# A dynamic convolution and SwiGLU kernel on one core: the part ahead of the loop recorded anew, in one fixed order for every engine

## The chip, the cores and the metric

The kernel runs on one core of a Trainium2 chip. Its time is the device time of one execution in microseconds (us), lower is better. The kernel before takes 1240.89 us as the median of 3 runs (1240.53 to 1242.09).

## The reference, cut to what matters

```python
# x (4, 4096, 192), weight_gen (4, 4096, 8, 7), float32
w = softmax(weight_gen, axis=-1)                      # 7 taps for each of 8 heads
x_pad = concat([zeros(B, 6, D), x], axis=1)
attn[b, s, h, :] = sum_k w[b, s, h, k] * x_pad[b, s + k, h, :]
x = attn.reshape(16384, 192)
xn = x / sqrt(mean(x * x, axis=-1) + 1e-6) * rms_g
g, val = xn @ w_gate, xn @ w_val                      # (192, 1536) each, float64 in memory
out = (g * sigmoid(g) * val) @ w_out                  # (1536, 192), float64 in memory
```

## The kernel before

**Blocks.** The 16384 tokens are cut into 32 blocks of 512 (4 tokens on each of 128 partitions). Four blocks share one load group: `xg` holds the group's tokens, `wt` its tap weights. For each block `conv` multiplies the shifted `xg` by a tap seven times (`tmp`) and sums (`acc`), takes the mean square (`junk`, `ssq`, `rs`), scales (`xn`) and splits the result into two 16-bit parts (`sp`). `trans` turns `sp` round with a transposing DMA into `tt`, and two more DMAs copy the halves of `tt` crosswise into `tu`. All DMAs but one small pair are issued by SyncE (SP), in one order.

**Stage 1 and stage 2.** `s1_mm(i, c)` is a chunk: 18 matmuls of TensorE (PE), which run in pairs, give 128 columns of gate (`pg`) and value (`pv`) for block i. ScalarE (ACT) takes the Silu of `pg` (`sg`), VectorE (DVE) multiplies by `pv` (`hf`), ACT and GpSimd (POOL) split `hf` into two 16-bit halves `hh`. There are 12 chunks in a block. `s2_mm` multiplies `hh` by the split `wo` into `po`; a block has 12 units of it, 4 chunks deep each. All PSUM tiles (`acc` on PE, `pt`, `pg`, `pv`, `po`) share eight buffers.

**Weights.** `w_gate` and `w_val` arrive as float64 in five slices k of 1, 2, 2, 3 and 4 chunks (loads `s0` to `s4`, buffers `rawa`, `rawb`), `w_out` in `wost`. `decode` makes float32 of them in four steps (`hf` scaled, `lo` shifted, two combining steps on DVE), ACT squares them, PE sums the squares into `pt`, DVE makes power-of-two scales, ACT and DVE then write the high and low 16-bit halves into `wm` and `wo`.

**What sets the order.** Everything up to the loop is recorded as the string `START` calls sixteen generators; a letter advances one of them, a dot issues the next load of `LOADS`. That covers the convolutions of blocks 0 to 2, all weights, 24 chunks (blocks 0 and 1) and stage 2 of block 0. In that part only SP is held to the recorded order (`manual_schedule`); the other engines' order is Tile's choice. The loop `for i in range(2, NB)` is written with DVE and PE held to the recorded order; the chunk (2, 0) is its first matmul.

Of the kernel before, what the change touches and what calls it, by code (L numbers as in the profile page):

```python
# [18 lines left out]
P = 128  # L19
R = 16  # L20
# [5 lines left out]
LOADS = ("w0", "w1", "s0", "x0", "s1", "x1", "s2", "s3", "x2", "s4")  # L26
START = (
    "..aaaa.aa.aa.aba.gapbbagab.gbcgbcabgcp.cpccpcgccacaccaca.daacaadgg.agabgegaadcgedddceddc"
    "gdggaagbggeeagaeeggebebgebbegfgbdagefbebdeeefecjbfiiggfdgfjjgegffekcfbgkkkbkdeekcpdfffjk"
    "ffbfjfphdjjdfjjjdjcjfjkjjdfcjjhhhdlhbehfhdhjfphldiplhkphjihkjpilkfmhjbilkhpkhjmhlhkhphkk"  # L30
    "ihidkhhiinphkmmnnhhnnphlnnhpmkphmkpkhjmlmjmkpkhpkmmhmphmhnmmolppllmoplmpmnppohpmpihohohp"
    "mhhohhhnomhnmhhnnhhnnmhhnmhhnhnnhnnnooooonni"
# [19 lines left out]
def tile_dynamic_conv_swiglu(  # L52
# [44 lines left out]
    ident = const.tile([P, P], F16, name="ident")  # L97
# [82 lines left out]
    normed = set()  # L180

    def conv(i, halves=False):

# [3 lines left out]
        parts = []  # L187
        b = 0
        for n, mul in ((2, nc.vector), (2, nc.gpsimd)) if halves else ((J, nc.vector),):
            pe = b > 0  # L190
            if pe:
                acc = ps1.tile([P, n, D], F32, tag="pr", name="acc")
            else:
                acc = p_c.tile([P, J, D], F32, tag="acc", name="acc")[:, 0:n, :]
            parts.append((b, b + n, mul, pe, acc))
            b += n
        for k in range(K):
            for a, b, mul, pe, acc in parts:
# [14 lines left out]
                if pe:
# [4 lines left out]
                elif k:  # L218
                    yield mul.tensor_tensor(out=acc, in0=acc, in1=dst, op=ALU.add)  # L219
        ssq = p_s.tile([P, J], F32, tag="ssq", name="ssq")  # L220
        junk = p_s.tile([P, D], BF16, tag="junk", name="junk")
        for a, b, mul, pe, acc in parts:
# [11 lines left out]
        for a, b, mul, pe, acc in parts:  # L234
            yield nc.vector.tensor_tensor(  # L235
                out=xn[:, a:b, :], in0=acc,
                in1=rs[:, a:b].unsqueeze(2).to_broadcast([P, b - a, D]), op=ALU.mult,
            )
        normed.add(i)
# [3 lines left out]
        low = nc.vector if i < 2 else nc.gpsimd  # L243
# [47 lines left out]
    def s1_evac(i, c, pair):  # L291
        pg, pv = pair
# [5 lines left out]
        if (i, c) in POOL_HIDDEN:  # L298
            nc.scalar.activation(out=hf_of[i, c], in_=pv, func=AF.Copy, scale=cs1[:, c : c + 1])
            yield nc.gpsimd.tensor_tensor(out=hf_of[i, c], in0=hf_of[i, c], in1=sg, op=ALU.mult)  # L300
        else:
            yield nc.vector.scalar_tensor_tensor(  # L302
                out=hf_of[i, c], in0=pv, scalar=cs1[:, c : c + 1], in1=sg, op0=ALU.mult, op1=ALU.mult
            )
# [28 lines left out]
    def s2_evac(i, t):  # L333
# [4 lines left out]
        nc.scalar.activation(out=lo, in_=pt[:, D:], func=AF.Identity, scale=so[:, 1:2])  # L338
# [14 lines left out]
    def decode(raw, how):  # L353
# [24 lines left out]
        if how[2] == "p":  # L378
            yield nc.scalar.activation(out=hf, in_=hf, func=AF.Sign)
            yield nc.gpsimd.tensor_tensor(out=hf, in0=hf, in1=lo.bitcast(F32), op=ALU.mult)  # L380
        else:
            yield nc.vector.scalar_tensor_tensor(
                out=hi, in0=hi, scalar=-0x80000000, in1=lo, op0=ALU.bitwise_and, op1=ALU.bitwise_or
            )
# [27 lines left out]
    def prep_gate_val(k):  # L412
        raw = raws.pop(k)
        a, b = (v * P for v in SL[k])
        n = b - a
        sq = p_d.tile([P, 3, 4 * P], BF16, tag="sq", name="sq", bufs=2)
        for m in range(3):
            yield from decode(raw[:, m, :], DECODE[k][m])
            yield nc.scalar.activation(
                out=sq[:, m, 0:n], in_=upper(raw[:, m, :]).bitcast(F32), func=AF.Square,  # L420
                scale=g_sb[:, m : m + 1], bias=eps, accum_out=ssq_w[:, k, m : m + 1],
            )
# [4 lines left out]
        sums = [
            [(by, ssq_w[:, k, m : m + 1]) for m in range(3)] for by in (rows[:, 0, :], rows[:, 1, :], same)
        ]
        for c in range(c0, c1):  # L430
            f = slice((c - c0) * P, (c - c0 + 1) * P)
            for h in range(2):
                sums.append([(sq[:, m, f], big[:, h : h + 1]) for m in range(3)])
        for q, terms in enumerate(sums):
            for t, (a_, b_) in enumerate(terms):
                nc.tensor.matmul(
                    pt[:, q : q + 1], a_, b_, start=(t == 0), stop=(t == len(terms) - 1)
                )
        scales(pt[:, 0:w], sc[:, o : o + w], isc[:, o : o + w], -XE)
# [5 lines left out]
        yield nc.vector.scalar_tensor_tensor(  # L445
# [3 lines left out]
        nc.gpsimd.tensor_tensor(  # L449
# [374 lines left out]
```

## Time and profile before

| what | value |
|---|---|
| median of 3 runs | 1240.89 us |
| the profiled execution, its own time | 1243.09 us |
| its span, first to last instruction | 1241.2 us |
| busy PE, DVE, ACT, POOL | 95%, 69%, 53%, 48% of the span |
| mean granted TensorE clock | 0.977 |

The profiled execution is 1.9 us longer than its span, and 2.2 us longer than the median. The busy shares are means over a start of some 150 us and a loop of some 1090 us, which have different limits; they have to be read stage by stage.

### The profile page before, as it was taken

How to read it: one execution, taken by the hardware profiler on the slowest of the kernel's cores; microseconds unless marked ns; L12 is line 12 of the kernel's file. 1: busy time of each engine (PE TensorE's matmuls, PEld its weight loads, DVE VectorE, ACT ScalarE, POOL GpSimd, SP SyncE). 2: the span in 40 equal slices, each digit the busy share in tenths (PEclk: the TensorE clock that was granted, in tenths of full speed). 3: DMA queues.
4: the chain of work that ended last, by engine and by line, in shares of the span. 5: the costliest groups of instructions: out<-in, count | busy, mean ns of one | idle time of the engine just before them, and what ended most of it. 6: DMA issues, size and time to landing. Idle time of an engine off the chain costs nothing.

```text
span 1241.2 us, 24390 instructions
## 1 busy us (share of the span) xinstructions
PE 1173.1 (95%) x10141; PEld 630.9 (51%) x10141; DVE 852.3 (69%) x1163; ACT 662.5 (53%) x1320; POOL 596.0 (48%) x525
## 2 busy tenths in 40 slices
PE   3468998989999999999999999999999999999998
PEld 1223554545555555555555555555555555555554
DVE  8893467667776677777776767777776777776532
ACT  3675553464455555555556555565556645555543
POOL 6335333444454455544555445544554555544442
PEclk9579999999999999999999999999999999999999
DMA  9421240111311133111310122111311111111010
GB/s 210 114 55 27 83 123 13 27 39 39 124 27 18 35 90 72 40 39 39 111 29 25 39 68 95 40 40 39 98 32 35 39 40 40 39 39 39 6 34 27
DMA packets 68086, 67.34 MB, mean 54 GB/s; under 512 B 52492, under 2 KB 55052, under 8 KB 67080
## 3 DMA queue, kind: packets, MB, share of 16 engines
q1 hardware_dynamic: 67912, 65.79, 19.7%
q8 instruction: 79, 1.29, 0.4%
q14 instruction: 31, 0.25, 0.1%
q0 software_dynamic: 64, 0.00, 0.0%
HBM read 28.03 MB, written 12.58 MB: 33 GB/s over the span
## 4 chain that ended last, share of the span: by engine, by line
PE 73%; issue 3%; DVE 2%; ACT 2%; POOL 1%; DVEq 0%; POOLq 0%
PE pg L283 46%; PE po L325 17%; PE po L328 8%; PE pv L283 2%; DVE hf L302 2%; ACT sg L296 1%; ACT hh L310 1%; POOL rs L232 0%; DVE tmp L210 0%; POOL hh L311 0%; DVE xn L235 0%; ACT sp L242 0%; ACT L296 0%; DVE ot L339 0%; ACT lo L338 0%
## 5 line engine op out<-in xcount | busy, mean ns | idle before, releaser
L311 POOL TENSOR_TENSOR hh<-hf,hh 128x512 f16<-128x512 f32 x384 | 448.3, 1168 | 457.0 <-ACT hh L310 457.0
L283 PEld LDWEIGHTS <-wm 64*128 64x128 f16 x6912 | 346.0, 95 | 448.0 <-issue 63.0
L283 PE MATMUL pg<-tt,wm 64*128 64x512 f16 x1920 | 489.7, 382 | 13.2 <-ACT sg L296 12.1
L302 DVE SCALAR_TENSOR_TENSOR hf<-pv,cs,sg 128x512 f32<-128x512 f32 x382 | 286.5, 750 | 301.8 <-ACT sg L296 210.9
L283 PE MATMUL pv<-tu,wm 64*128 64x512 f16 x1920 | 484.7, 381 | 0.0
L310 ACT ACTIVATE hh<-hf 128x512 f16<-128x512 f32 x384 | 242.0, 630 | 356.6 <-DVE hf L302 354.7
L283 PE MATMUL pv<-tt,wm 64*128 64x512 f16 x1536 | 401.1, 382 | 13.7 <-ACT sg L296 6.4
L283 PE MATMUL pg<-tu,wm 64*128 64x512 f16 x1536 | 400.2, 381 | 0.7 <-DMA tu<-tt 0.6
L325 PE MATMUL po<-wo,hh 128*128 128x384 f16 x1536 | 379.3, 326 | 0.7 <-DVE wo L496 0.7
L328 PE MATMUL po<-wo,hh 128*128 128x192 f16 x1536 | 376.4, 246 | 0.0
L296 ACT ACTIVATE sg<-pg,isc 128x512 f32<-128x512 f32 x384 | 257.6, 671 | 24.6 <-PE pv L283 24.6
L325 PEld LDWEIGHTS <-hh 128*128 128x128 f16 x1536 | 150.2, 98 | 111.2 <-issue 13.6
L219 DVE TENSOR_TENSOR acc<-acc,tmp 128x768 f32<-128x768 f32 (+1 forms) x192 | 197.6, 1029 | 0.8
L210 DVE TENSOR_TENSOR tmp<-xg,wt 128x768 f32<-128x768 f32 (+1 forms) x192 | 187.9, 981 | 0.0
L328 PEld LDWEIGHTS <-hh 128*128 128x128 f16 x1536 | 150.3, 98 | 0.7 <-issue 0.7
L339 DVE SCALAR_TENSOR_TENSOR ot<-po,so,lo 128x192 f32<-128x192 f32 x128 | 52.8, 413 | 59.7 <-ACT lo L338 59.3
L232 POOL TENSOR_TENSOR rs<-rs,mhalf 128x4 f32<-128x4 f32 x32 | 42.7, 1333 | 86.6 <-DVE rs L228 86.1
L338 ACT ACTIVATE lo<-po,so 128x192 f32<-128x192 f32 x128 | 49.8, 409 | 46.6 <-PE po L328 42.0
L242 ACT ACTIVATE sp<-xn 128x768 f16<-128x768 f32 x32 | 27.0, 844 | 76.1 <-DVE xn L235 76.1
L224 ACT ACTIVATE junk<-acc 128x192 bf16<-128x192 f32 x128 | 46.0, 360 | 34.5 <-DVE acc L219 32.1
L244 POOL TENSOR_TENSOR sp<-xn,sp 128x256 f16<-128x256 f32 x30 | 21.9, 731 | 62.3 <-ACT sp L242 62.3
L247 POOL TENSOR_TENSOR sp<-xn,sp 128x512 f16<-128x512 f32 x30 | 50.1, 1670 | 0.0
(94 smaller groups left out, 348.3 us busy)
## 6 DMA issues: line engine op xcount, KB each, us to landing
tu<-tt SPq DMA_DIRECT2D x64, 192.0 KB, 2.9
out_dram<-ot SPq DMA_DIRECT2D x31, 384.0 KB, 3.0
xg<-in_x_dram SPq DMA_DIRECT2D x7, 1536.0 KB, 8.1
wt<-in_weight_gen_dram SPq DMA_DIRECT2D x7, 448.0 KB, 8.2
wost<-in_moe_w_out_dram SPq DMA_DIRECT2D x1, 2304.0 KB, 9.2
xg<-in_x_dram SPq DMA_DIRECT2D x4, 576.0 KB, 4.2
xg<-in_x_dram SPq DMA_DIRECT2D x4, 504.0 KB, 5.3
xg<-in_x_dram SPq DMA_DIRECT2D x2, 384.0 KB, 11.3
```

What stands on the lines that cost most here:

```text
L210: yield mul.tensor_tensor(out=dst.rearrange("p j (h c) -> p (j h) c", h=H), in0=xk, in1=wk, op=ALU.mult)
L219: yield mul.tensor_tensor(out=acc, in0=acc, in1=dst, op=ALU.add)
L247: yield low.tensor_tensor(out=sp[:, :, D + L :], in0=xn[:, :, 0:P], in1=sp[:, :, 0:P], op=ALU.subtract)
L283: mm = nc.tensor.matmul(pt, wm[h, grp, wpart, f], xT[i][half != m][h, q], start=(n == 0), stop=(n == 8))
L296: yield nc.scalar.activation(out=sg, in_=pg, func=AF.Silu, scale=isc[:, o : o + 1])
L302: yield nc.vector.scalar_tensor_tensor(out=hf_of[i, c], in0=pv, scalar=cs1[:, c : c + 1], in1=sg, op0=ALU.mult, op1=ALU.mult)
L310: yield nc.scalar.activation(out=hid[i][:, 0, c, :], in_=hf, func=AF.Copy)
L311: yield nc.gpsimd.tensor_tensor(out=hid[i][:, 1, c, :], in0=hf, in1=hid[i][:, 0, c, :], op=ALU.subtract)
L325: mm = nc.tensor.matmul(pt, hid[i][:, 0, n, c], wo[:, n, :], start=(n == 0), stop=False,)
L328: nc.tensor.matmul(pt[:, 0:D], hid[i][:, 1, n, c], wo[:, n, 0:D], start=False, stop=(n == NC - 1),)
L338: nc.scalar.activation(out=lo, in_=pt[:, D:], func=AF.Identity, scale=so[:, 1:2])
L339: nc.vector.scalar_tensor_tensor(out=ot[i][:, t, :], in0=pt[:, 0:D], scalar=so[:, 1:2], in1=lo, op0=ALU.mult, op1=ALU.add,)
```

## The change

For blocks 0 and 1 `conv` no longer halves the block between DVE (products and sums) and POOL (products, summed by PE). DVE makes all seven products over the whole block, and PE sums both halves through the identity matrix `ident32`, two matmuls of 128x384 in float32 for each tap. `decode` has no POOL steps any more, and one fixed list says which of its steps ACT takes. The generators become finer: each third of a weight slice, the high parts, the low parts and the two halves of each evacuation are streams of their own, so that one letter of `START` is about one instruction of one engine. All five engines are held to the recorded order. Two chunks whose `hf` product went to POOL go to DVE; the low split of block 2 goes from POOL to DVE. The loop's code is the same.

```diff
-LOADS = ("w0", "w1", "s0", "x0", "s1", "x1", "s2", "s3", "x2", "s4")
+LOADS = ("w0", "x0", "s0", "s1", "w1", "s2", "x1", "s3", "s4", "x2", "wo")
 START = (
-    "..aaaa.aa.aa.aba.gapbbagab.gbcgbcabgcp.cpccpcgccacaccaca.daacaadgg.agabgegaadcgedddceddc"
...
+    "...aa.aa.a.a..AAdffdffAfeedAeidiAhhighdihiAhAbllbkjebglgAbAAAbeAbksjgAgoBAsmoAmBtttAnTnA"
...
+DECODE = "aa da dd ad aa aa aa aa aa aa aa aa aa aa ad dd aa aa aa".split()
...
-    def conv(i, halves=False):
+    def conv(i, pe=False):
...
-        for n, mul in ((2, nc.vector), (2, nc.gpsimd)) if halves else ((J, nc.vector),):
...
+        if pe:
+            halves = [ps1.tile([P, n, D], F32, tag="pr", name="acc") for _ in range(2)]
+            parts = ((0, n, halves[0]), (n, J, halves[1]))
...
+        for k in range(K):
...
+            yield nc.vector.tensor_tensor(
+                out=dst.rearrange("p j (h c) -> p (j h) c", h=H), in0=xk, in1=wk, op=ALU.mult
+            )
             if pe:
...
+                for a, b, acc in parts:
                     nc.tensor.matmul(
                         acc.rearrange("p j d -> p (j d)"), ident32,
-                        dst.rearrange("p j d -> p (j d)"), start=(k == 0), stop=(k == K - 1),
+                        dst[:, a:b, :].rearrange("p j d -> p (j d)"),
+                        start=(k == 0), stop=(k == K - 1),
                     )
...
-        low = nc.vector if i < 2 else nc.gpsimd
+        low = nc.vector if i < 3 else nc.gpsimd
...
-        if (i, c) in POOL_HIDDEN:
-            nc.scalar.activation(out=hf_of[i, c], in_=pv, func=AF.Copy, scale=cs1[:, c : c + 1])
-            yield nc.gpsimd.tensor_tensor(out=hf_of[i, c], in0=hf_of[i, c], in1=sg, op=ALU.mult)
...
-            eng = nc.vector if how[0] == "d" else nc.gpsimd
-            yield eng.tensor_single_scalar(out=hf, in_=hf, scalar=2.0**-112, op=ALU.mult)
+            yield nc.vector.tensor_single_scalar(out=hf, in_=hf, scalar=2.0**-112, op=ALU.mult)
...
-        if how[2] == "p":
-            yield nc.scalar.activation(out=hf, in_=hf, func=AF.Sign)
-            yield nc.gpsimd.tensor_tensor(out=hf, in0=hf, in1=lo.bitcast(F32), op=ALU.mult)
...
+        "t": each((high_gate_val, k, m) for k in range(NS) for m in range(3)),
+        "T": each((low_gate_val, k, m) for k in range(NS) for m in range(3)),
...
+        "S": each((s1_mm, i, c) for i, c in both),
+        "O": each((s2_mm, 0, *unit(u)) for u in range(NC)),
+    }
+    streams["E"], streams["F"] = in_two(s1_evac, both)
+    streams["H"], streams["L"] = in_two(s1_split, both)
...
-    with tc.manual_schedule(engines={mybir.EngineType.SP}):
+    with tc.manual_schedule(engines={
+        mybir.EngineType.SP, mybir.EngineType.DVE, mybir.EngineType.PE,
+        mybir.EngineType.Activation, mybir.EngineType.Pool,
+    }):
         for ch in START:
```

The first place is DVE at the first convolution. Before, from its first product on, the half block is multiplied and added here (`tmp`, `acc`), while POOL multiplies the other half:

```order
L210 TENSOR_TENSOR acc<-xg,wt 128x384
L210 TENSOR_TENSOR tmp<-xg,wt 128x384 x2
L219 TENSOR_TENSOR acc<-acc,tmp 128x384
L210 TENSOR_TENSOR acc<-xg,wt 128x384
L219 TENSOR_TENSOR acc<-acc,tmp 128x384
L210 TENSOR_TENSOR tmp<-xg,wt 128x384 x2
```

Now, on the same engine and from the same product on:

```order
L191 TENSOR_TENSOR tmp<-xg,wt 128x768 x2
L342 TENSOR_SCALAR rawa<-rawa 128x128
L351 TENSOR_SCALAR rawa<-rawa 128x128
L354 SCALAR_TENSOR_TENSOR rawa<-rawa 128x128
L357 SCALAR_TENSOR_TENSOR rawa<-rawa 128x128
L191 TENSOR_TENSOR tmp<-xg,wt 128x768
```

The sums are gone from DVE, its products are twice as wide, and the decoding steps of slice 0 stand between them.

The second place is SP from the load of slice 3 (`rawb`, 384 wide) to the load of `w_out`. Before, all slices are issued ahead of the first transpose:

```order
L409 DMA rawb<-in_moe_w_val_dram 64x3x384
L151 DMA xg<-in_x_dram 128x1536
L409 DMA rawb<-in_moe_w_gate_dram 64x3x512
L409 DMA rawb<-in_moe_w_val_dram 64x3x512
L259 DMA_TRANSPOSE tt<-sp 128x12x128
L158 DMA wt<-in_weight_gen_dram 128x896
L262 DMA tu<-tt 64x1536
L263 DMA tu<-tt 64x1536
L466 DMA wost<-in_moe_w_out_dram 128x12x192
```

Now the fourth slice (512 wide) and the rest of `xg` stand behind block 0's transpose and its two copies:

```order
L384 DMA rawb<-in_moe_w_val_dram 64x3x384
L149 DMA wt<-in_weight_gen_dram 128x896
L242 DMA_TRANSPOSE tt<-sp 128x12x128
L245 DMA tu<-tt 64x1536
L246 DMA tu<-tt 64x1536
L384 DMA rawb<-in_moe_w_gate_dram 64x3x512
L384 DMA rawb<-in_moe_w_val_dram 64x3x512
L142 DMA xg<-in_x_dram 128x1536
L452 DMA wost<-in_moe_w_out_dram 128x12x192
```

So the block's own transpose no longer has the last slice in front of it, and the last slice waits for it.

The third place is SP a little later, between the copies of block 1 and the first store. Before, block 2's transpose stands ahead of the next group's load (`xg`, 128x1152 and 128x3072):

```order
L259 DMA_TRANSPOSE tt<-sp 128x12x128
L262 DMA tu<-tt 64x1536
L263 DMA tu<-tt 64x1536
L142 DMA xg<-in_x_dram 128x1152
L151 DMA xg<-in_x_dram 128x3072
L347 DMA out_dram<-ot 128x768
```

Now the load stands ahead of it:

```order
L133 DMA xg<-in_x_dram 128x1152
L142 DMA xg<-in_x_dram 128x3072
L242 DMA_TRANSPOSE tt<-sp 128x12x128
L245 DMA tu<-tt 64x1536
L246 DMA tu<-tt 64x1536
L326 DMA out_dram<-ot 128x768
```

The load of the next group has moved ahead of block 2's transpose and copies. In both programs this load goes into the buffer of `wost`, so it waits until the last `wo` is written.

## Rows read from the trace of the kernel before

**Rows 1.** Windows: us, then each engine's busy time (instructions), granted PE clock, DMA share, GB/s.

```profile
0.00:53.30 53.30, 17.56 (x112) 8.54 (x112) 44.58 (x100) 22.54 (x69) 28.90 (x43) 0.79 0.71 161
53.30:89.80 36.50, 26.09 (x182) 10.32 (x179) 35.91 (x60) 25.52 (x54) 13.97 (x11) 0.75 0.30 87
89.80:147.50 57.70, 51.34 (x396) 25.87 (x396) 23.17 (x41) 34.69 (x73) 27.41 (x24) 0.91 0.17 52
147.50:345.00 197.50, 186.01 (x1585) 102.70 (x1585) 139.78 (x174) 96.90 (x188) 82.61 (x72) 0.98 0.20 60
400.00:1200.00 800.00, 800.00 (x7084) 429.79 (x7081) 560.72 (x723) 436.34 (x850) 403.62 (x342) 1.00 0.18 48
```

**Rows 2.** Waits of PE from 0 to 147.5: us in total, times, longest.

```profile
PE pt L436 <- ACT sq L419: 19.2, 7, 9.3
PE acc L214 <- POOL tmp L210: 16.5, 7, 13.8
```

**Rows 3.** Timeline of PE: start, duration, first matmuls of chunks and of stage 2.

```profile
53.35 0.61 PE L283 MATMUL pg<-tt,wm 64*128 64x512 f16 x1
...
57.17 0.63 PE L283 MATMUL pg<-tt,wm 64*128 64x512 f16 x1
...
59.38 0.38 PE L283 MATMUL pg<-tt,wm 64*128 64x512 f16 x1
...
61.33 0.38 PE L283 MATMUL pg<-tt,wm 64*128 64x512 f16 x1
...
89.89 0.39 PE L283 MATMUL pg<-tt,wm 64*128 64x512 f16 x1 [1.01 <-ACT wm L456]
...
147.57 0.39 PE L283 MATMUL pg<-tt,wm 64*128 64x512 f16 x1
...
155.44 0.34 PE L325 MATMUL po<-wo,hh 128*128 128x384 f16 x1
...
167.31 0.39 PE L283 MATMUL pg<-tt,wm 64*128 64x512 f16 x1
```

**Rows 4.** Timeline of DVE: start, duration.

```profile
18.14 2.35 DVE L210 TENSOR_TENSOR tmp<-xg,wt 128x384 f32<-128x384 f32 x2
...
43.20 0.54 DVE L210 TENSOR_TENSOR tmp<-xg,wt 128x384 f32<-128x384 f32 x1
43.67 0.55 DVE L375 SCALAR_TENSOR_TENSOR rawb<-rawb 128x384 int32<-128x384 int32 x1
...
127.52 3.03 DVE L496 SCALAR_TENSOR_TENSOR wo<-wost,ws,wo 128x192 f16<-128x192 f32 x7 [0.86 <-ACT wo L493]
```

**Rows 5.** Groups of POOL from 0 to 40: count, busy us, mean ns, idle before.

```profile
L210 POOL TENSOR_TENSOR tmp<-xg,wt 128x384 f32<-128x384 f32 x14 | 15.3, 1119 | 0.6 <-DMA xg<-in_x_dram 0.6
```

**Rows 6.** Timeline of SP's issues: start, duration.

```profile
17.30 0.60 SPq L409 DMA_DIRECT2D rawb<-in_moe_w_val_dram  x1
...
41.28 1.53 SPq L259 DMA_TRANSPOSE tt<-sp  x1
...
45.61 0.60 SPq L263 DMA_DIRECT2D tu<-tt  x1
```

**Rows 7.** DMA issues from 0 to 160: KB each, us from issue to landing.

```profile
xg<-in_x_dram SPq DMA_DIRECT2D x1, 1536.0 KB, 8.9
tu<-tt SPq DMA_DIRECT2D x6, 192.0 KB, 3.0
...
rawb<-in_moe_w_val_dram SPq DMA_DIRECT2D x1, 768.0 KB, 21.9
```

**Rows 8.** Timeline of PE: one float32 matmul of 128x384 (two records) each.

```profile
18.99 0.91 PE L214 MATMUL acc<-tmp,ident 128*128 128x384 f32 x2
...
32.81 1.63 PE L214 MATMUL acc<-tmp,ident 128*128 128x384 f32 x2
```

**Rows 9.** Groups of DVE from 400 to 1200: count, busy us, mean ns, idle before.

```profile
L302 DVE SCALAR_TENSOR_TENSOR hf<-pv,cs,sg 128x512 f32<-128x512 f32 x276 | 207.0, 750 | 206.2 <-ACT sg L296 132.1 <-issue 74.1
L219 DVE TENSOR_TENSOR acc<-acc,tmp 128x768 f32<-128x768 f32 x132 | 136.8, 1036 | 0.3
```

More of the change, by code (lines that the diff above doesn't have):

```diff
@@ L220, in conv @@
         ssq = p_s.tile([P, J], F32, tag="ssq", name="ssq")
         junk = p_s.tile([P, D], BF16, tag="junk", name="junk")
-        for a, b, mul, pe, acc in parts:
+        for a, b, acc in parts:
             for j in range(a, b):
@@ L233, in conv @@
         xn = p_c.tile([P, J, D], F32, tag="xn", name="xn", bufs=1)
[L234 to L235 removed]
+        for a, b, acc in parts:
+            mul = nc.vector.tensor_tensor(
                 out=xn[:, a:b, :], in0=acc,
@@ L410, in load_gate_val, with square_gate_val, scale_gate_val @@
         raws[k] = raw
[L412 to L422, printed above, removed]
+    sqs = {}
+    def square_gate_val(k, m):
+        n = (SL[k][1] - SL[k][0]) * P
+        raw = raws[k][:, m, :]
+        yield from decode(raw, DECODE[3 * k + m])
+        if k not in sqs:
+            sqs[k] = p_d.tile([P, 3, 4 * P], BF16, tag="sq", name="sq", bufs=2)
+        yield nc.scalar.activation(
+            out=sqs[k][:, m, 0:n], in_=upper(raw).bitcast(F32), func=AF.Square,
+            scale=g_sb[:, m : m + 1], bias=eps, accum_out=ssq_w[:, k, m : m + 1],
+        )
+    def scale_gate_val(k):
         c0, c1 = SL[k]
+        sq = sqs.pop(k)
         w = 3 + 2 * (c1 - c0)
@@ L426, in prep_gate_val @@
         pt = ps1.tile([P, TB], F32, tag="pr", name="pt")
[L427 to L435, printed above, removed]
+        for q, by in enumerate((rows[:, 0, :], rows[:, 1, :], same)):
+            for m in range(3):
                 nc.tensor.matmul(
-                    pt[:, q : q + 1], a_, b_, start=(t == 0), stop=(t == len(terms) - 1)
+                    pt[:, q : q + 1], by, ssq_w[:, k, m : m + 1], start=(m == 0), stop=(m == 2)
                 )
+        for c in range(c1 - c0):
+            for m in range(3):
+                nc.tensor.matmul(
+                    pt[:, 3 + 2 * c : 5 + 2 * c], sq[:, m, c * P : (c + 1) * P], big,
+                    start=(m == 0), stop=(m == 2),
+                )
+        yield
         scales(pt[:, 0:w], sc[:, o : o + w], isc[:, o : o + w], -XE)
@@ L613, in s2_unit, with each, in_two, head @@
         if u % 3 == 2:
-            s2_evac(i, u // 3)
+            run(s2_evac(i, u // 3))
         return mm
-    done = {}
-    def need(ch, n):
-        while done.get(ch, 0) < n:
-            step(ch)
+    def each(steps):
+        for f, *args in steps:
+            r = f(*args)
+            if hasattr(r, "__next__"):
+                yield from r
+            else:
+                yield
+    def in_two(make, keys):
+        begun = {}
+        def head():
+            for key in keys:
+                begun[key] = make(*key)
+                yield next(begun[key])
+        def tail():
+            for key in keys:
+                run(begun.pop(key))
+                yield
+        return head(), tail()
@@ L748, in tile_dynamic_conv_swiglu @@
+    assert not left and all(next(gen, 0) == 0 for gen in streams.values())
     if NG > 1:
```

272 lines of the change are left out of this document (91 added, 181 removed).

## The prediction, made before the changed kernel ran

> **What bounds the kernel now.** I read the busy time by stretches first, since the page's means mix a start and a loop [rows 1]. From 400 to 1200 us PE is busy all 800 us at full clock: the loop is bound by PE, nothing there is left to win, and the change does not touch it. From 147.5, where the loop's first chunk starts, to 345 PE loses 197.5 - 186.0 = 11.5 us: in its first blocks VectorE is late. The rest is lost ahead of the loop. Of the first 147.5 us PE works 17.6 + 26.1 + 51.3 = 95.0, and part of that at half clock (0.79, 0.75 and 0.91 granted).
>
> What it waits for stands in the waits of that stretch [rows 2]: 19.2 us for squares of weights (ACT), 16.5 us for POOL's products. Neither engine is itself full there. DVE is: 44.6 of the first 53.3 us, and 35.9 of the next 36.5 [rows 1]. ACT's squares wait for decoded weights, which DVE makes. So DVE's work decides when the first and the ninth chunk can run.
>
> The timeline of PE gives four marks [rows 3]: the first chunk starts at 53.35, the ninth (the first one that needs weight slice 4) at 89.89, the loop at 147.57, and the end comes 1241.2 - 147.57 = 1093.6 after that. A chunk takes 57.17 - 53.35 = 3.82 us at half clock and 61.33 - 59.38 = 1.95 at full, stage 2 of a block 167.31 - 155.44 = 11.87. At full clock the way from first chunk to loop would be 24 x 1.95 + 11.87 = 58.7 us; it takes 94.2. The start is worth up to 35 us there, and the 53 us ahead of it more.
>
> Why is DVE so full? Two of its products of half a block beside POOL's take 2.35 us, one alone 0.54 [rows 4]. POOL multiplies 14 times, 15.3 us in all, 1.12 each [rows 5]: a DVE operation beside one of POOL's takes about as long as POOL's. The Trainium skill says in "SBUF — State Buffer", section "SBUF: two separate sides", that a DVE operation with two SBUF inputs and a GpSimd one that reads SBUF lock each other out for a whole instruction. Rows 4 and 5 agree.
>
> **The change, step by step.** I carry the four marks over to the new order.
>
> *To the first chunk.* POOL's 15.3 us and the doubled DVE operations go. DVE makes seven products of 128x768 for a block: 0.95 each, from 2 x 0.54 less one start (in the loop operations of that size average 1.04 beside POOL [rows 9]). It loses all sums: before, six adds and seven products of half width, each at 0.54 to 1.2. Loads are the other limit. Before, 7164 KB are down at 17.3 + 21.9 = 39.2 us [rows 6, 7], 183 KB/us. The first tokens now stand right behind the first taps, with 1068 KB down at some 6 to 9 us instead of behind 1788; the eighth product, block 1's first, needs the second tokens, 3710 KB, at 20 to 22. From 8.5 us DVE's list up to block 0's last low split has nine such products (8.6 us) and some forty decoding and softmax steps of 0.1 to 0.75 (about 9.6, sized by width from the 0.55 of a 384-wide step [rows 4]); the squares, root and scaling of block 0 add about 3 of waiting. That is 29.7 for the transpose, which was issued at 41.28 [rows 6]. To the end of its two copies it took 45.61 + 3.0 - 41.28 = 7.3 [rows 6, 7]. Slice 4 no longer stands before it. The first chunk: **37.0** instead of 53.35, 16.3 less. Bounds 33 (no waiting) and 43 (the loads set each step).
>
> *PE's price.* Sums on PE are not free. A tap of a block is two matmuls; one takes 0.91 alone at full clock and 1.63 at half, and their difference of 0.72 is its time without the latency [rows 8], so 1.44 us for a tap, 2.6 to 2.9 at half clock. For block 0 that follows the products with little to spare: `tmp` has two buffers, so at half clock PE would hold up DVE from the third product on. For block 1 ten of the fourteen stand between the first chunk and the fourth, where PE is on the path: 7.2 us.
>
> *First to ninth chunk.* PE has three chunks and ten sums up to block 1's last sum: 3 x 1.95 + 7.2 = 13.1, plus about 4 for its first microseconds at half clock (3.82 for 1.95, twice). That sum is there at 54. Behind it ACT, now in a fixed order, must do block 1's squares, three squares of slice 4 and six high parts (5.5 us) before the third Silu at 60; DVE follows with its products, the scales of slice 4 and the low parts at 67.5. The ninth chunk: **67.5** instead of 89.89; the stretch is 30.5 against 36.5, 6.0 less. Slice 4 is issued at about 35, behind the copies, and is down at about 45 (1536 KB at 183 KB/us, 8.4, and two for the latency): ahead of its first use at 47, so its move costs nothing; if it comes later, every microsecond over two counts. Bounds 26 and 38.
>
> *Ninth chunk to the loop.* Sixteen chunks and stage 2 need 16 x 1.95 + 11.87 = 43.1 at full clock; before, 57.7. What stands beside them on DVE has grown, since `w_out`'s decoding and block 2's convolution now lie here: up to `wo` 17 products `hf` (12.8), 12 operations of the convolution (12.4) [rows 9], 8 steps on `wost` (as `hf`, 6.0), and the small ones, about 33 when the start-to-start overlap is taken off (43.67 - 43.20 = 0.47 for an operation of 0.54 [rows 4]). So `wo` starts at 67.5 + 33.5 = 101, where PE would be ready at 67.5 + 15 x 1.95 = 96.8: 4.2 to 5 lost. Twelve `wo` take 12 x 0.43 = 5.2 [rows 4], alongside PE's first units.
>
> Here the third place of the order costs. The next group's `xg` waits for the last `wo`, at 106, and needs 8.9 [rows 7]; block 2's transpose, ahead of it before, is behind it now, and its low split stands on DVE behind the first `ot`. Transpose and copies are ready some 18.5 after `wo` starts, PE is done with stage 2 after 14.2: 3.5 to 4 lost (nothing if the transfers share the queue well). The stretch is 43.1 + 5 + 4 = 52, the loop starts at **119.5** instead of 147.57: 5.7 less. Bounds 45 and 64.
>
> *The loop.* Same code, same order on PE and DVE; its early losses of 11.5 come from DVE's order behind `hf`, not from the start's end. 0, bounds -4 and +4.
>
> **Sum:** -16.3 - 6.0 - 5.7 = -28 us. Against the profiled execution's 1243.1 that is 1215.1; the median lies 2.2 lower, so 1240.9 - 28 = **1213 us**.
>
> **Rivals.**
>
> *POOL's lock moves (0.12).* POOL's 24 splits of 1.2 us for blocks 0 and 1 now fall on a full DVE. Its 14 operations of the convolution would take 1.9 instead of 0.95 if each met one: 13 us more, so `wo` at 114 and about **1226**. Against it: in the loop, with POOL busy 404 of 800 us, such adds average 1.04, not 1.9 [rows 1, 9].
>
> *The start opens further (0.06).* If loads are quicker, the ninth chunk runs at 60 and neither `wo` nor the transpose holds PE, the loop starts at 60 + 43.1 = 103 and the time is about **1197**. For it: DVE loses more work than I count on. Against it: ACT has some 33 us of its own in the last stretch.
>
> *PE stays at half clock (0.05), the slower side.* From first chunk to loop PE has 58.7 + 7.2 = 66 us at full clock, 132 at half. From 37 on, with 12 us of waits, the loop would start at 37 + 12 + 66(1 + f), f the share of that work at half clock: 115 for none, 148 for f = 0.5, 181 for all; slower than before above one half. At f = 0.65 the time is **1252**. For it: between 53.3 and 89.8 the clock was 0.75 with PE working 26 of 36.5 us, about half at 1.2 GHz [rows 1]. Against it: with 51 of 57.7 us at work it was 0.91, and PE's waits get shorter. The Trainium skill ("TensorE: Matmul & The Clock Gate", section "What's actually happening") has throttling as the default state, which activity releases; the trace agrees in rows 3, 3.82 to 1.95 within one chunk of steady work. By that rule this rival needs waits as frequent as before.
>
> *The order is broken by one late item (0.02): no change.* With every engine in a fixed order, a late `wost` stands in ACT's queue before slice 4's high parts and holds Silu, chunks and DVE. It is due at about 55 and needed at 60; it takes 28 + 5 us of delay to lose all the gain.
>
> **How the numbers follow.** My forecast holds 0.75: gains of 17 to 39, 1202 to 1224, from the bounds of the three stretches, which will not all fall on one side. 8 in 10 are within **1202 to 1226**, with the contention case at its upper end. A difference of 0.2% (2.5 us) is about what a measurement of this kernel can tell. Faster: 0.75 + 0.12 + 0.06 = 0.93; the same 0.02; slower 0.05.
>
> **What would show it.** The first chunk near 37, POOL nearly idle up to 45, DVE products of 128x768 at 0.95 in the first 40 us; the ninth chunk near 67 behind a third Silu that waited for block 1's squares; `wo` near 101; a PE wait for `tt` or `tu` at the loop's start; the same 11 to 12 us of PE waits in the 200 us behind that. I am wrong on the cause if DVE's products there are still near 1.2 a half block, if the first chunk comes after 45, or if the loop loses other than before.

## The result, and the profile after

The changed kernel takes 1220.68 us (median of 4 runs, 1219.51 to 1221.45) against 1241.04 for the one before (4 runs): ratio 0.9834, 95% interval 0.9817 to 0.9851, 20.4 us less. The direction and the range (1202 to 1226) held; the gain is three quarters of the 28 us forecast. The profiled execution took 1221.45 us with a span of 1219.7, 21.5 less than the span before.

The marks of the prediction are the first matmuls of the first chunk, of the ninth and of the loop, and the end of the span. The table has the first of them and the stretches between:

| mark or stretch (us) | before | predicted | after |
|---|---|---|---|
| first chunk | 53.35 | 37.0 | 35.78 |
| first to ninth chunk | 36.54 | 30.5 | 32.75 |
| ninth chunk to loop | 57.68 | 52 | 53.87 |
| loop to end of span | 1093.6 | 1093.6 | 1097.3 |

Windows of after, cut at its own marks; columns as in [rows 1]:

```profile
0.00:35.70 35.70, 18.27 (x78) 9.85 (x79) 27.16 (x64) 19.11 (x56) 5.43 (x23) 0.86 0.77 164
35.70:68.50 32.80, 28.99 (x202) 13.16 (x203) 26.61 (x55) 23.39 (x50) 6.32 (x8) 0.84 0.55 157
68.50:122.40 53.90, 47.48 (x399) 23.99 (x396) 47.27 (x68) 40.71 (x93) 30.29 (x22) 0.97 0.26 63
122.40:320.00 197.60, 185.93 (x1547) 100.63 (x1549) 136.54 (x170) 94.36 (x183) 81.25 (x71) 0.96 0.21 62
400.00:1175.00 775.00, 775.00 (x6856) 417.97 (x6854) 543.63 (x702) 422.50 (x827) 391.50 (x331) 1.00 0.18 48
```

The loop from 400 us is as full of PE as before. Ahead of the first chunk DVE works 27.2 us instead of 44.6, and POOL, whose products [rows 5] are gone, 5.4 instead of 28.9. The third row is the one to stop at: DVE is now busy 47.3 of 53.9 us (before, 23.2 of 57.7), so it is as full there as PE.

The five largest waits of PE up to the loop; columns as in [rows 2]:

```profile
PE acc L196 <- DVE tmp L191: 13.8, 4, 8.0
PE pv L266 <- DVE hf L281: 3.9, 3, 3.1
PE pt L409 <- ACT sq L396: 3.3, 2, 3.1
PE pv L266 <- DMA tu<-tt: 2.5, 1, 2.5
PE pg L266 <- DVE wm L443: 1.5, 1, 1.5
```

The 19.2 us for squares have shrunk to 3.3. The 13.8 for products lie ahead of the first chunk, where PE has nothing else. What costs is new: `hf` (3.1 in one piece), block 0's copies (`tu`), for which PE stands inside the first chunk, the low parts of slice 4 (`wm`), and, on the far side of the loop's start, block 2's transposed tiles. PE's timeline at the marks:

```profile
68.53 0.38 PE L266 MATMUL pg<-tt,wm 64*128 64x512 f16 x1
...
70.56 0.39 PE L266 MATMUL pg<-tt,wm 64*128 64x512 f16 x1 [1.45 <-DVE wm L443]
...
122.40 0.39 PE L266 MATMUL pg<-tt,wm 64*128 64x512 f16 x1 [0.66 <-DMA tt<-sp]
...
125.15 0.37 PE L266 MATMUL pv<-tu,wm 64*128 64x512 f16 x1 [1.50 <-DMA tu<-tt]
125.99 0.37 PE L266 MATMUL pg<-tu,wm 64*128 64x512 f16 x1 [0.46 <-DMA tu<-tt]
```

Stage 2 of block 1 starts at 134.47, so the loop's first four chunks take 12.1 us where they took 7.9 (147.57 to 155.44 in [rows 3]). These 4.2 us, less 0.5 by which the rest of the loop is shorter, are the +3.7 of the table's last line.

### The profile page after: what moved, and what is told of

Read it like the earlier page. It is cut to its first block, busy times and chain, and to the rows that moved or that the text cites. A ratio compares the mean times of both kernels' runs of the same rounds, so it can differ in the third digit from the quotient of the medians.

```text
span 1219.7 us, 24318 instructions
## 1 busy us (share of the span) xinstructions
PE 1176.7 (96%) x10133; PEld 633.1 (52%) x10133; DVE 849.4 (70%) x1147; ACT 662.9 (54%) x1322; POOL 569.2 (47%) x499
## 4 chain that ended last, share of the span: by engine, by line
PE 74%; issue 3%; DVE 2%; ACT 2%; POOL 1%; DVEq 0%; POOLq 0%
PE pg L266 47%; PE po L304 17%; PE po L307 8%; PE pv L266 2%; DVE hf L281 2%; ACT sg L279 1%; ACT hh L289 1%; POOL rs L215 0%; DVE tmp L191 0%; POOL hh L290 0%; DVE xn L218 0%; ACT sp L225 0%; ACT L279 0%; DVE ot L318 0%; ACT lo L317 0%
## 5 line engine op out<-in xcount | busy, mean ns | idle before, releaser
L290 POOL TENSOR_TENSOR hh<-hf,hh 128x512 f16<-128x512 f32 x384 | 452.8, 1181 | 437.6 <-ACT hh L289 437.6
L191 DVE TENSOR_TENSOR tmp<-xg,wt 128x768 f32<-128x768 f32 x194 | 193.0, 996 | 7.0 <-PE acc L196 5.6
L202 DVE TENSOR_TENSOR acc<-acc,tmp 128x768 f32<-128x768 f32 x180 | 188.4, 1047 | 0.8
L215 POOL TENSOR_TENSOR rs<-rs,mhalf 128x4 f32<-128x4 f32 x32 | 43.1, 1346 | 110.2 <-DVE rs L211 109.7
## 6 DMA issues: line engine op xcount, KB each, us to landing
xg<-in_x_dram SPq DMA_DIRECT2D x2, 384.0 KB, 10.2
```

The source lines that it names most:

```text
L191: yield nc.vector.tensor_tensor(out=dst.rearrange("p j (h c) -> p (j h) c", h=H), in0=xk, in1=wk, op=ALU.mult)
L202: yield nc.vector.tensor_tensor(out=acc, in0=acc, in1=dst, op=ALU.add)
L290: yield nc.gpsimd.tensor_tensor(out=hid[i][:, 1, c, :], in0=hf, in1=hid[i][:, 0, c, :], op=ALU.subtract)
```

## The experiments

Each kernel is the changed one with the edit shown. "The theory" is the first case of an expectation, "the rival" the other. Three things limit a fine comparison. Runs of one kernel spread over 0.5 to 5.6 us. The marks come from one execution of each kernel, which need not be a middle one: that of e2 is the slowest of its four, that of e6 the fastest. And the first chunk came between 33.3 and 35.8 us in the profiled executions that have the same code up to there (after, e1, e3, e7, e10); the later load of slice 0 landed 6.4 to 8.4 us after its issue in them. So stretches from the first chunk on are compared beside the times. The kernel before, run beside each group on the same chip, had medians of 1240.6 to 1242.2; the ratios given are against these. The marks of all runs:

| run | time, median us | first chunk | to ninth | to loop | loop to end |
|---|---|---|---|---|---|
| after | 1220.68 | 35.78 | 32.75 | 53.87 | 1097.3 |
| e1 load behind the transpose | 1215.36 | 33.33 | 32.64 | 53.14 | 1093.2 |
| e2 four `tmp` | 1218.14 | 34.52 | 30.79 | 56.66 | 1097.2 |
| e3 no POOL splits | 1211.07 | 34.44 | 33.32 | 44.58 | 1097.2 |
| e4 free order | 1226.89 | 34.66 | 33.10 | 63.35 | 1093.6 |
| e5 POOL multiplies half | 1220.14 | 34.05 | 31.00 | 55.12 | 1097.1 |
| e6 slice 4 first | 1220.28 | 35.06 | 32.23 | 54.27 | 1094.1 |
| e7 = e1, four splits late | 1214.72 | 33.51 | 32.98 | 54.03 | 1092.1 |
| e8 convolution of before | 1220.47 | 38.22 | 29.73 | 55.45 | 1095.3 |
| e9 load order of before | 1225.15 | 38.58 | 33.31 | 54.47 | 1097.2 |
| e10 = e1, loop's products held | 1211.45 | 35.00 | 32.76 | 49.74 | 1093.2 |
| e11 = e4 and e8 | 1232.81 | 43.13 | 28.42 | 65.70 | 1093.2 |
| e12 = e10, e2, two `hf` earlier | 1210.73 | 34.76 | 30.79 | 50.92 | 1093.2 |

**e1: the load of the next group behind block 2's transpose.** Its two lines move from behind the start into its fixed order.

```diff
         for ch in START:
             go(ch)
+        load_x(1)
+        load_w(1)
...
-    if NG > 1:
-        load_x(1)
-        load_w(1)
```

> The load of the next group is issued behind block 2's transpose, its copies and the first store, as before the change. If the load's 2 MB in the same queue make the transpose and its copies late, the transpose lands some 4.4 us after its issue at 114.6 instead of 7.8, the copies are down at about 122, PE does not wait for tu and its clock does not fall, so the loop's first four chunks take 7.9 us instead of 12.1: 4 to 5 us less, about 1216. Rival: the transpose is late by its own issue (it stands behind the low split that ends at 114.5), then a wait of 1 to 2 us at the loop's start stays and the time is 1219 to 1220. Second rival: the late load holds block 4's convolution, and PE loses later what it gains here: 1221.

Measured: ratio 0.9795 (0.9780 to 0.9809), 5.3 us below after; by the marks from the first chunk on, 4.9. SP's issues in after, start and duration:

```profile
111.41 1.01 SPq L142 DMA_DIRECT2D xg<-in_x_dram  x1
114.58 3.83 SPq L242 DMA_TRANSPOSE tt<-sp  x1
122.41 0.47 SPq L245 DMA_DIRECT2D tu<-tt  x1
```

and in e1:

```profile
112.02 1.42 SPq L242 DMA_TRANSPOSE tt<-sp  x1
115.71 0.46 SPq L245 DMA_DIRECT2D tu<-tt  x1
```

From the transpose's issue to the first copy, which waits for it, 7.8 us have become 3.7. The loop's first four chunks take 7.9 us again, at full clock, and loop to end is 1093.2. The first rival (late by its own issue) falls, and so does the second: the load, now issued at 120.6, is missed nowhere.

**e2: four buffers for `tmp`** (`bufs=4` in its tile).

> tmp has four buffers instead of two, nothing else. If DVE's waits for the sums on PE (5.6 us in three waits) set the ninth chunk, they go, DVE's list runs 3 to 5 us earlier, PE's wait for the low parts at 70.6 goes, and the time falls by 2 to 4 us to about 1218. Rival: PE's own list, chunks and sums in a fixed order, ends block 1's sums at 55 as now and the third Silu at 59; what DVE gains it waits for later at the Silu, and the time stays within 1 us of 1220.7.

Measured: ratio 0.9823 (0.9808 to 0.9837); the interval takes in the ratio of after, 0.9834. The median, 1218.14, lies where the theory had it, 2.5 us below after, but the marks, those of the slowest of the four runs (1220.95), do not show that gain. DVE waited for PE's sums in after:

```profile
DVE tmp L191 <- PE acc L196: 5.6, 3, 4.2
```

In e2 1.1 us of them are left, and the ninth chunk comes 2.0 us sooner after the first, but the loop does not: 87.4 us from first chunk to loop against 86.6. Ahead of the ninth chunk DVE now waits for ACT instead, 2.1 us for `wm`, 1.3 for `sg` and 0.8 for `rawb`, and `wo` starts 70.2 us behind the first chunk in both. In this execution the rival is right for the end of the stretch, the theory for the ninth chunk; what made the other three runs faster is not shown.

**e3: no low splits on POOL for blocks 0 and 1.**

```diff
-        yield nc.gpsimd.tensor_tensor(
-            out=hid[i][:, 1, c, :], in0=hf, in1=hid[i][:, 0, c, :], op=ALU.subtract
-        )
+        if i > 1:
+            nc.gpsimd.tensor_tensor(
+                out=hid[i][:, 1, c, :], in0=hf, in1=hid[i][:, 0, c, :], op=ALU.subtract
+            )
+        yield
...
-                pt[:, 0:D], hid[i][:, 1, n, c], wo[:, n, 0:D], start=False, stop=(n == NC - 1),
+                pt[:, 0:D], hid[i][:, int(i > 1), n, c], wo[:, n, 0:D], start=False, stop=(n == NC - 1),
```

> POOL's 24 low splits of blocks 0 and 1 are left out; stage 2 of these two blocks reads the high half in their place, so the output differs there. If POOL's splits slow DVE between 60 and 107, its doubled operations (1.71 for a wost step, 0.99 each for the low parts of slice 4) fall to 0.55 to 0.75, PE's waits at 70.6 and 101.1 shrink by 3 to 4 us, wo starts 4 us earlier, and the time falls by 3 to 5 us to about 1217. Rival: DVE has slack there, PE waits on the chain from Silu to hf, and the time stays within 1.5 us of 1220.7.

Measured: ratio 0.9756 (0.9741 to 0.9771), 9.6 us below after, twice what the theory asked for; all of it in the third stretch (44.6 instead of 53.9). Groups of DVE from 56 to 108 us in after (count, busy us, mean ns, idle before):

```profile
L281 DVE SCALAR_TENSOR_TENSOR hf<-pv,cs,sg 128x512 f32<-128x512 f32 x19 | 13.6, 737 | 0.0
L191 DVE TENSOR_TENSOR tmp<-xg,wt 128x768 f32<-128x768 f32 x7 | 9.4, 1356 | 0.0
...
L354 DVE SCALAR_TENSOR_TENSOR wost<-wost 128x576 int32<-128x576 int32 x4 | 5.5, 1385 | 0.0
L357 DVE SCALAR_TENSOR_TENSOR wost<-wost 128x576 int32<-128x576 int32 x4 | 4.3, 1063 | 0.0
L443 DVE SCALAR_TENSOR_TENSOR wm<-rawb,gs,wm 128x512 f16<-128x512 f32 x3 | 3.0, 1036 | 0.0
```

and in e3:

```profile
L281 DVE SCALAR_TENSOR_TENSOR hf<-pv,cs,sg 128x512 f32<-128x512 f32 x22 | 15.9, 736 | 0.0
L191 DVE TENSOR_TENSOR tmp<-xg,wt 128x768 f32<-128x768 f32 x7 | 6.5, 941 | 0.0
...
L359 DVE SCALAR_TENSOR_TENSOR wost<-wost 128x576 int32<-128x576 int32 x4 | 3.0, 744 | 0.0
L356 DVE SCALAR_TENSOR_TENSOR wost<-wost 128x576 int32<-128x576 int32 x4 | 3.0, 742 | 0.0
L445 DVE SCALAR_TENSOR_TENSOR wm<-rawb,gs,wm 128x512 f16<-128x512 f32 x3 | 2.1, 739 | 0.0
```

The product `hf`, which reads PSUM and SBUF, takes the same in both. Operations that read two SBUF tiles take 1.4 to 1.9 times as long beside POOL's splits: 7 x 0.42 + 4 x 0.64 + 4 x 0.32 + 3 x 0.30 = 7.7 us in these four groups alone. Leaving out the splits also frees the `hf` buffers sooner: DVE's one wait for that, 1.1 us in after, is gone. In the third stretch DVE is busy 37.1 of 44.6 us, so the rival's slack is there only without the splits. The Trainium skill ("SBUF — State Buffer", section "SBUF: two separate sides") says that a DVE operation with two SBUF inputs and a GpSimd one that reads SBUF exclude each other, for a whole instruction. These rows agree as to which operations are stretched, the unchanged `hf` included; means do not show that it is for whole instructions.

**e4: free order.** Up to the loop only SP keeps the recorded order.

```diff
-    with tc.manual_schedule(engines={
-        mybir.EngineType.SP, mybir.EngineType.DVE, mybir.EngineType.PE,
-        mybir.EngineType.Activation, mybir.EngineType.Pool,
-    }):
+    with tc.manual_schedule(engines={mybir.EngineType.SP}):
```

> Only SP is held to the recorded order up to the loop, as before the change; PE, DVE, ACT and POOL stand in the order that Tile chooses. If the moved work (sums on PE, nothing of convolution and decoding on POOL) makes the gain, the loop still starts at 122 to 128 and the time is 1220 to 1226. Rival: the computed order makes it; then Tile's order loses most of the gain, the loop starts beyond 135 and the time is over 1232.

Measured: ratio 0.9893 (0.9877 to 0.9910), 1226.89 us, between theory and rival. The first chunk comes as early as in the computed order; the order is worth 9.5 us in the third stretch (63.4 against 53.9). Block 2's transpose stands well ahead of the load here, so the loop starts without a wait, and the fair partner is e1, 11.5 us faster.

**e5: POOL multiplies the second half again**, DVE only the first; PE sums both.

```diff
+            dk = dst.rearrange("p j (h c) -> p (j h) c", h=H)
+            m = n * H if pe else J * H
+            nc.vector.tensor_tensor(out=dk[:, 0:m], in0=xk[:, 0:m], in1=wk[:, 0:m], op=ALU.mult)
+            if pe:
+                nc.gpsimd.tensor_tensor(out=dk[:, m:], in0=xk[:, m:], in1=wk[:, m:], op=ALU.mult)
```

> In the convolutions of blocks 0 and 1 POOL multiplies the second half of the block again, DVE only the first; PE sums both halves as now, the order of the letters is the same. If the two engines hold each other up, each of DVE's products stays near 1.1 to 1.2 us though it is half as wide (0.55 alone), the decoding steps beside POOL's products lengthen too, the first chunk comes 1 to 4 us later and the time is 1221 to 1226. Rival: POOL's help is free; DVE saves 7 x 0.4 = 2.8 us for each block, the first chunk comes at 32 to 33 and the ninth 3 us or more earlier, 1215 to 1218.

Measured: ratio 0.9831 (0.9818 to 0.9845), no difference from after. DVE's products up to 34 us in e5, then in after:

```profile
L193 DVE TENSOR_TENSOR tmp<-xg,wt 128x384 f32<-128x384 f32 x10 | 8.0, 816 | 1.0 <-DMA xg<-in_x_dram 1.0
```

```profile
L191 DVE TENSOR_TENSOR tmp<-xg,wt 128x768 f32<-128x768 f32 x10 | 9.4, 951 | 1.4 <-DMA xg<-in_x_dram 1.3
```

Half the width costs 0.82 instead of 0.95. POOL's help saves DVE 1.4 us there, and the decoding steps beside it lose about as much: three `rawa` steps of 128x128 average 0.69 us in e5 and 0.29 in after (1.2 us), and six of 128x256 take 0.53 instead of 0.42 each (0.6). Neither the theory's time came nor the rival's: the engines do hold each other up, and it takes back what POOL contributes.

**e6: slice 4 ahead of block 0's transpose** (one dot of `START` moved up).

> Slice 4 is issued ahead of block 0's transpose, as before the change. If its 1536 KB stand in the way of the transpose and the copies, these land later by 2 to 6 us and the first chunk comes at 37 to 41, 1222 to 1226; the decoding of slice 4 is ahead of its need either way. Rival: the transpose and its copies share the queues well enough, or DVE and PE had waits to give there; the time stays within 1.5 us of 1220.7.

Measured: ratio 0.9831 (0.9816 to 0.9847), no difference, though the runs lie between 1217.4 and 1223.0. From the transpose's issue to the first copy it took 5.3 us instead of 4.5; the rival is right to within the spread. In the profiled execution, the fastest of the four, the loop's first four chunks took 8.8 us and not 12.1, with block 2's transpose issued 4.1 us behind the load instead of 3.2; whether that is the edit's doing is not shown.

**e7: e1, and the low splits of block 1 that stood ahead of the last `wo` put behind it** (four letters `L` of `START`, twelve buffers for `hf`).

> As e1 (next group's load behind the transpose), with POOL's low splits of block 1 that stood ahead of the last wo put behind it (four of them; hf has twelve buffers). If POOL's splits slow DVE one by one, four of sixteen gone give a quarter of what the run without splits gave, 2 us: 1213. Rival: DVE's loss there comes from the queue that POOL is (hf waits for a buffer); then twelve buffers give the same gain only at the wait for hf at 101, below 1 us, and POOL's backlog behind wo delays block 1's stage 2: 1215 to 1217.

Measured: ratio 0.9792 (0.9779 to 0.9805), 0.6 us below e1, less than the spread: inconclusive. PE's wait for `hf` at 98 fell from 3.1 to 2.1 us, but two waits of 0.8 for `wo` came in.

**e8: the convolution of before in the computed order** for blocks 0 and 1: the first half multiplied and summed on DVE, the second multiplied on POOL and summed on PE.

```diff
-            halves = [ps1.tile([P, n, D], F32, tag="pr", name="acc") for _ in range(2)]
-            parts = ((0, n, halves[0]), (n, J, halves[1]))
+            acc0 = p_c.tile([P, J, D], F32, tag="acc", name="acc")[:, 0:n, :]
+            acc1 = ps1.tile([P, n, D], F32, tag="pr", name="acc")
+            parts = ((0, n, acc0), (n, J, acc1))
...
```

> Blocks 0 and 1 are convolved as before the change (DVE multiplies and sums one half, POOL multiplies the other and PE sums that), at the places of the new order. Against e5 this gives DVE twelve sums of half a block more, at 0.55 alone and up to 1.2 beside POOL: 6.6 to 14 us over the two blocks, half of it ahead of the first chunk. If the sums on DVE were what kept it full, the first chunk comes 3 to 7 us later than in e5's order and the time is 1224 to 1232. Rival: DVE waits anyway in that stretch (for loads before the first chunk, 5.6 us for PE's sums behind it, which now go); the time stays at 1219 to 1222, and the gain of the first stretch comes from what stands ahead of block 0, not from how it is summed.

Measured: ratio 0.9830 (0.9817 to 0.9844), no difference. The first chunk comes 4.2 us later than in e5, as the theory had it (3 to 7), and 2.4 later than in after. But from there to the ninth it takes 29.7 instead of 32.8, and DVE's 5.6 us of waits for PE's sums are gone: for the time the rival is right.

**e9: the first loads in the order of before.** Slice 4 and the last tokens keep their new places.

```diff
-LOADS = ("w0", "x0", "s0", "s1", "w1", "s2", "x1", "s3", "s4", "x2", "wo")
+LOADS = ("w0", "w1", "s0", "x0", "s1", "x1", "s2", "s3", "s4", "x2", "wo")
```

> The loads stand in the order of before the change (all taps, slice 0, then the first tokens), nothing else is changed. If the tokens' place behind the first taps is worth something, the first product starts some 4 us later than at 6.9, behind slice 0's decoding in place of ahead of it; DVE's waits of 5.8 us for loads grow by 1 to 3 us and so does the time: 1222 to 1224. Rival: slice 0 lands earlier by as much, DVE's sum of waits is the same and the time stays within 1.5 us of 1220.7.

Measured: ratio 0.9866 (0.9851 to 0.9881), 4.5 us above after. The first product starts at 11.88 instead of 6.92 (DVE waits 5.7 us for `xg`), the first chunk at 38.58. The theory, with 1222 to 1224, had 1.3 to 3.3.

**e10: e1, and two products of block 3 held back.** The loop's DVE instructions keep their order among themselves, but the first of them may slip in among the start's. In after's order of DVE (the numbers tell tiles apart: `tmp_1027` is block 2's, `acc_1388` and `tmp_1390` are block 3's):

```
L281 SCALAR_TENSOR_TENSOR hf_601<-pv_509,cs1_100,sg_567 128x512
L191 TENSOR_TENSOR acc_1388<-xg_133,wt_131 128x768
L281 SCALAR_TENSOR_TENSOR hf_606<-pv_536,cs1_100,sg_571 128x512
...
L191 TENSOR_TENSOR tmp_1027<-xg_133,wt_131 128x768
L191 TENSOR_TENSOR tmp_1390<-xg_133,wt_131 128x768
L281 SCALAR_TENSOR_TENSOR hf_1052<-pv_940,cs1_100,sg_988 128x512
```

The same rows in the timeline of after:

```profile
63.00 1.92 DVE L191 TENSOR_TENSOR acc<-xg,wt 128x768 f32<-128x768 f32 x1
...
96.67 3.73 DVE L191 TENSOR_TENSOR tmp<-xg,wt 128x768 f32<-128x768 f32 x2
100.33 0.73 DVE L281 SCALAR_TENSOR_TENSOR hf<-pv,cs,sg 128x512 f32<-128x512 f32 x1
```

The second stands right ahead of the `hf` for which PE waits 3.1 us at 101. A tile that occupies the buffer until block 2's low split is written holds both back:

```diff
...
+            done += ch == "C"
+            if ch == "C" and done in (1, 19):
+                hold.append(p_c.tile([P, J, D], F32, tag="acc", name="hold"))
+            if ch == "C" and done == 22:
+                for t in hold:
+                    nc.vector.memset(t[:, 0, 0:1], 0.0)
```

> As e1, and the first two products of block 3, which the loop records and which stand among the start's DVE rows (at 63.0 for 1.92 us, and at 96.7 in a pair of 3.73 us), are held back behind block 2's low split: their buffer is kept by a tile that is let go there. If DVE is full in that stretch and sets wo, wo comes 3 to 4 us earlier, PE's waits at 68 for the low parts and at 98.6 for hf lose 1.5 and 2 us, and the time falls from e1's 1215.4 to about 1212. Rival: PE waits for the chain of Silu there, or the two products are missed later in the loop's first blocks, where DVE is late anyway: 1214.5 to 1216.

Measured: ratio 0.9756 (0.9743 to 0.9770), 3.9 us below e1: the theory. The third stretch is 3.4 shorter, `wo` starts at 101.8 (103.4 in e1, whose first chunk was 1.7 earlier), and loop to end is 1093.2 as in e1, so nothing is missed later. PE's waits changed otherwise than expected. Those for the low parts fall by 1.4, those for `hf` only from 3.9 to 3.4, as they move to other products. The rest is the clock; windows from the ninth chunk on, e1, then e10 (columns as in [rows 1]):

```profile
66.00:73.50 7.50, 5.74 (x33) 1.90 (x31) 7.50 (x11) 5.21 (x13) 1.36 (x1) 0.77 0.47 105
```

```profile
67.70:75.20 7.50, 7.17 (x63) 3.16 (x60) 7.50 (x12) 5.65 (x14) 0.00 (x0) 1.00 0.27 65
```

Behind the wait for the low parts part of e1's stretch ran at 1.2 GHz, a loss of 0.23 x 7.5 = 1.7 us; without the wait it ran at full clock.

**e11: e4 and e8 together.**

> The free order of e4 and the convolution of before (e8) together: what is left of the change is the order of the loads, the decoding without POOL and the finer recording. If the convolution's form matters only where no computed order works round it, this run is 5 to 10 us behind e4's 1226.9: 1232 to 1237. Rival: it is worth as little here as in the computed order, then 1225 to 1229, and what e4 keeps of the gain comes from loads, decoding and recording.

Measured: ratio 0.9938 (0.9922 to 0.9955), 1232.81 us, the theory. In the free order the first chunk waits until 43.13 with the convolution of before and until 34.66 with the new one. PE's waits up to 72 us in e11 look like those of before:

```profile
PE acc L195 <- POOL tmp L191: 19.4, 3, 11.2
PE pt L428 <- ACT sq L415: 14.2, 6, 3.8
```

**e12: e10, four `tmp`, and two `hf` products moved up on DVE** (two letters `F` of `START`).

> As e10, with four buffers for tmp and two hf products moved ahead of the rows that hold them on DVE: one ahead of two decoding steps of w_out (it started at 83.8, its Silu was done at 80.3), one ahead of block 2's last product (it started at 95.9, its Silu was done at 94.2). If PE's waits of 1.7 and 1.2 us at these places are what is left on its path, the time falls by 2 to 3 us from e10's 1211.5 to about 1209. Rival: what is taken off these waits comes back at the next hf or at wo, since DVE is full; 1211 to 1212.

Measured: ratio 0.9760 (0.9745 to 0.9774), 1210.73 us. Its distance to e10 is within the spread; the time lies between theory and rival, nearer to the rival. It is, with e10, the fastest version with the whole computation: about 10 us below the changed kernel.

## Why the prediction was right or wrong

**First chunk (-16.3 forecast, -17.6 measured).** The size held, in part by luck. My sum has the first matmul behind the end of block 0's two copies, at 37.0. In after SP issues the transpose and the copies so:

```profile
31.34 1.54 SPq L242 DMA_TRANSPOSE tt<-sp  x1
35.80 0.53 SPq L245 DMA_DIRECT2D tu<-tt  x1
36.38 0.59 SPq L246 DMA_DIRECT2D tu<-tt  x1
```

and PE starts so:

```profile
35.78 0.37 PE L266 MATMUL pg<-tt,wm 64*128 64x512 f16 x1 [0.48 <-DMA tt<-sp]
...
39.49 0.58 PE L266 MATMUL pv<-tu,wm 64*128 64x512 f16 x1 [2.47 <-DMA tu<-tt]
```

The transpose was issued 1.6 us later than the 29.7 of the sum, but the chunk starts on `tt` alone and stands for the copies inside it, until 39.5. So 2.5 us that I had ahead of this mark fall behind it.

The reason held only in part. I put the gain to POOL's products, the doubled operations and the sums leaving DVE. e5 and e8 put these back at the new places and the time stayed; with e8's first chunk at 38.22, 15.1 of the 17.6 us remain. The pairs show what gains:

| medians, us | convolution of before | new convolution |
|---|---|---|
| free order | 1232.81 (e11) | 1226.89 (e4) |
| computed order | 1220.47 (e8) | 1220.68 (after) |

By these times the new form is worth 5.9 us where Tile orders the engines and nothing in the computed order; the order is worth 12.3 with the old form and 6.2 with the new. They hold unequal waits at the loop's start, though: its first four chunks take 7.9 us in e11 and e4, 9.9 in e8 and 12.1 in after. An estimate without them, from these four stretches, has after at 1216.5 and e8 at 1218.5: then the form is still worth 2 us in the computed order, and the order 14 with the old form and 10 with the new. By the marks either alone brings the first chunk forward, from 43.1 to 34.7 or to 38.2. The 7.8 us from before (1240.6 beside e11) to e11, and 10.2 of the 17.6 at the first mark, are left to load order, decoding without POOL and the finer recording. The order of the first loads is worth 4.5 in the computed order (e9). The other two were not separated, so the cause of this part stays open.

**Slice 4's move costs nothing:** right. But "slice 4 no longer stands before it" wins nothing that can be measured either (e6).

**First to ninth chunk (-6.0 forecast, -3.8 measured).** The stretch took 32.75 us against 30.5. The step that failed is the one above: the 2.5 us for block 0's copies lie in it, not ahead of it. A second cost is missing at "ten of the fourteen": I charged PE's time for block 1's sums to PE, but not the 5.6 us for which DVE stands still with two `tmp` buffers. With four the stretch is 30.79 (e2); most of that gain is clock, granted 0.84 in after and 0.89 in e2 (0.16 x 32.8 less 0.11 x 30.8 us). So other terms of the sum were some 2 us too large; which ones the runs do not show. The third Silu came at 59.4 (60 forecast).

**Ninth chunk to loop (-5.7 forecast, -3.8 measured).** `wo` started at 106.0, not 101. DVE at the two ends, in after:

```profile
67.23 1.71 DVE L354 SCALAR_TENSOR_TENSOR wost<-wost 128x576 int32<-128x576 int32 x1
68.86 2.96 DVE L443 SCALAR_TENSOR_TENSOR wm<-rawb,gs,wm 128x512 f16<-128x512 f32 x3
...
105.98 4.34 DVE L489 SCALAR_TENSOR_TENSOR wo<-wost,ws,wo 128x192 f16<-128x192 f32 x10 [0.46 <-ACT wo L484]
```

From the end of slice 4's low parts (71.8) to `wo` it took 34.2, against 33.5 forecast; the low parts were late. The first step that failed is "the low parts at 67.5": between 62 and 71.8 DVE did a product of block 3 that I had not listed (1.92), a step on `wost` at 1.71 and the three low parts at 2.96 instead of 2.1, each stretched by POOL. The runs put sizes to both: POOL's splits 9.6 us (e3), block 3's two products 3.9 (e10). The two overlap, as the splits stretch those products too. The sum also took PE at full clock here; behind the wait for the low parts it was not (e10). Part of the 9.6 was in my sum without being named, as I took averages of the loop, 1.04 for an operation that takes 0.94 alone.

**The load ahead of the transpose (3.5 to 4 forecast).** Mechanism right: 5.3 (e1). The place was not: I booked it ahead of the mark, and the copies' wait lies behind it, as at block 0. There it is 1.5 + 0.5 of waits and a spell at half clock, which the sum does not have.

**The loop (0 forecast, +3.7).** That spell and those waits. With the load behind, the rest is 1093.2 (e1, e10), so "the loop loses the same" holds.

**The rivals.** "POOL's lock moves" is half true. The mechanism is there, with `tmp` products at 1.36 instead of 0.94 and not at 1.9, and it is worth 9.6 where I gave it 13. But `wo` did not slip to 114: the products are not doubled throughout, and `hf` is not touched. The start did not open further, as DVE is full to `wo`. PE did not stay at half clock (0.97 in the third stretch), and no late item broke the order.

## What to carry to other kernels

When the work moved is off the path in the new order, its form costs little: put the old form back in the new order before crediting either. In a stretch where DVE is full, list every DVE row in the final order, also rows of later code that slip in, and cost those with two SBUF inputs by rows beside POOL's work, not by a mean over the loop. And look at what the transfer queue holds ahead of the last small transfer before a stage.

## What the runs showed of the hardware

Some short waits of PE cost more than their length. Windows of after around the waits at 125 us, columns as in [rows 1]:

```profile
122.40:126.80 4.40, 2.43 (x18) 0.95 (x20) 0.31 (x1) 0.00 (x0) 0.85 (x1) 1.00 0.63 179
126.80:130.30 3.50, 3.50 (x21) 1.51 (x18) 1.61 (x2) 1.32 (x2) 0.98 (x1) 0.52 0.02 5
130.30:134.40 4.10, 4.10 (x40) 1.98 (x36) 2.48 (x4) 1.98 (x4) 1.33 (x2) 0.99 0.00 0
```

After waits of 0.7, 1.5 and 0.5 us PE works without a pause for 3.5 us at a granted clock of 0.52, its 1.2 GHz level, and then at full again. That loses 0.48 x 3.5 = 1.7 us, nearly as much as the 2.0 of waits behind the loop's start. e1 takes the waits away, and the spell goes with them. The wait for the low parts had such a spell behind it too, and e10 shows it gone with the wait. Not every wait does this: after PE's longest between first chunk and loop, 3.1 us for `hf` at 98, the granted clock stays at full in after,

```profile
97.00:104.00 7.00, 3.94 (x45) 1.92 (x43) 7.00 (x7) 3.78 (x12) 6.25 (x4) 1.00 0.01 2
```

and so it does in e8 behind waits of 1.1 and 0.4 us for `tu` at the loop's start. Which waits lower the clock the runs do not settle.

POOL's work is stretched as well: its splits, 1181 ns on average over the span of after, average 1590 from 56 to 108 us, where DVE is full. That DVE's operations with two SBUF inputs hold them up fits this; no run took those away to show it.
